# Row numbers between two layers at a wider pitch, output scatters declared independent, and products done by token half

## Chip, cores and metric

The kernel runs on 1 core of one Trainium2 chip. The metric is device time in microseconds (us), lower is better; each run gives the time of one execution. The profile is of one further execution, and its own time stands beside its span below.

## What is computed

Three layers in a row on 24,576 tokens of 256 numbers (8 sequences of 3,072), all float32:

```python
X = np.fft.rfft(x, axis=1)
Y = X * (filt_r + 1j * filt_i)[None, :, :]
x = np.fft.irfft(Y, n=3072, axis=1).reshape(24576, 256)

e_idx = np.argmax(x @ w_gate, axis=1)
for e in range(8):
    mask = e_idx == e
    h = np.maximum(x[mask] @ w1[e], 0.0)
    out[mask] = gate_w[mask, None] * eom[mask, e, None] * (h @ w2[e])

h = np.maximum(out @ w_in, 0.0)
return h * h @ w_out
```

The first is a filter in the frequency domain. The second is a layer of 8 experts (256 to 1,024 to 256), of which each token takes one. The third is a dense layer (256 to 2,048 to 256). The weights `w_in` and `w_out` of the third come as 64-bit numbers and are decoded on the chip.

## The kernel before

**Filter and routing** (up to about 750 us). The transform is done with matmuls; its last step also gives the routing scores. VectorE works out each token's expert and its place in that expert's list, and GpSimd scatters the token's row number to that place in one of four tables in HBM (`scatter`, L405: 128 numbers of 4 bytes in one DMA, each to its own place; the four tables are taken in turn). Tokens go to HBM as `yd`.

**Expert layer** (about 680 to 1965 us). The lists are cut into 62 tiles of one expert each: 41 wide ones of 512 tokens and 21 narrow ones of 256 (`width`). For each tile SP reads the list from the tables (`start_t`), GpSimd gathers the tokens (`gather`, L739), VectorE scales them (`scale_x`, L765), TensorE turns them (`turn_x`, L777, whose result ScalarE and VectorE split in two parts at L781 and L782), and `up` and `down` do the two products. All float32 products are done as three products of high and low parts. `load_w` brings expert weights from HBM, 512 KB for each quarter of a tile. The result of a tile goes to HBM transposed (`ytd`, L822), and with it the row numbers of its tokens (`idsc`, L823), so that the third layer can put each token's result in its row. A wide tile's 512 numbers are written as 128 runs of 4 (16 bytes), since slot 4p + c holds the number of token c * 128 + p. A narrow tile's 256 are written one by one, since its slot c * 128 + p holds token c * 128 + p. In both cases the numbers lie next to each other, 4 bytes apart.

**Decoding** runs beside the expert layer. `decode_all` is a generator that `step_1` moves on by one piece at six of every eight steps (L979). Each call of `decode` has SP load 256 KB of raw weights (`raw`, L612) and then works on VectorE, from L617 on. SP and VectorE take their instructions in program order, so a late load holds up all that stands behind L617 on VectorE.

**Dense layer** (about 1965 us to the end). 48 tiles of 512 columns of `ytd`, each in 8 units. `load_t` reads a tile and its row numbers (`ix`) more than one tile ahead; `split_t` splits the tile in high and low parts on ScalarE and VectorE (L859, L860) and forms sums of it (L868). The row numbers are read as four runs per partition; because narrow tiles were written in the other order, `split_t` takes the columns of the tiles from number 41 on with a step of four (`by`, L855). `up2` and `down2` do the products, interleaved in four parts per unit. `down2` sums a tile's four blocks of 128 tokens in two banks, `py0` for the first two blocks (k = 0) and `py1` for the others (k = 1):

```python
for m in range(24):
    i, k, c, n = m // 12, m // 6 % 2, m // 3 % 2, m % 3
```

so in each unit the banks take turns in groups of six matmuls. In a tile's last unit ScalarE copies a bank out (L934) when its last matmul, m = 17 or 23, is done, and GpSimd scatters its two blocks to their rows of the output (L937: 128 rows of 1 KB in a DMA). All of these scatters write the tensor `out`, and the framework, which cannot know that the rows differ, makes each wait until the one before has landed.

Of the kernel before, what the change touches and what calls it, by code (L numbers as in the profile page):

```python
# [11 lines left out]
F32 = mybir.dt.float32  # L12
F32R = mybir.dt.float32r
BF16 = mybir.dt.bfloat16
I32 = mybir.dt.int32
# [7 lines left out]
NT = B * S  # L23
# [8 lines left out]
TT = 512  # L32
# [9 lines left out]
NWIDE = KP + NTILE_L  # L42
# [58 lines left out]
def spectral_moe_kernel(ctx: ExitStack, tc: tile.TileContext, x, filt_r, filt_i, w_gate, w_og, w1, w2,  # L101
                        w_in, w_out, c_ma, c_mi, c_mb, c_mb2, c_sg, c_cum, out):
    nc = tc.nc
    ctx.enter_context(tc.manual_schedule())

    const = ctx.enter_context(tc.tile_pool(name="const", bufs=1))
# [2 lines left out]

    NTAB = 4  # L110
    ytd = dram.tile([D, NT + TT], F32, name="ytd")
    idsc = dram.tile([NT + TT, 1], I32, name="idsc")
    tab = [dram.tile([128 * TP, 1], I32, name=f"tab{i}") for i in range(NTAB)]
    tabv = [t.rearrange("(p c) o -> p (c o)", p=128) for t in tab]


# [36 lines left out]

    fft = ctx.enter_context(ExitStack())
    const.tile([128, 72], F32, name="pad")
    pl = {"xsm": ctx.enter_context(tc.tile_pool(name="xsm", bufs=2, side="right"))}
    right = lambda stack, name, bufs, **kw: stack.enter_context(tc.tile_pool(name=name, bufs=bufs, side="right", **kw))
    pl["xsm"].tile([128, 24], F32, name="xpad", bufs=1)  # L160
# [542 lines left out]
    slot, k = [], 0  # L703
# [102 lines left out]
    def down(t, f):  # L806
        hh, hl = H.pop((t, f))
        w = width[t]
        h2, l2 = (a[:, 1] for a in W[t, f // 2])
        if f == 0:  # L810
            Y[t] = [p[:, 0:w] for p in py_tiles(t)]
        for h in range(2):
            for i, (a, b) in enumerate(((h2, hh), (h2, hl), (l2, hh))):
                nc.tensor.matmul(Y[t][h], a[:, f % 2, h * 128:(h + 1) * 128], b,  # L814
                                 start=f == 0 and i == 0, stop=f == NF - 1 and i == 2)
        if f == NF - 1:
            yo = pl["yop1"].tile([128, 2, TT], F32, name="yt")[:, :, 0:w]
            for h, p in enumerate(Y.pop(t)):
                nc.scalar.copy(yo[:, h, :], p)
            c = cols.pop(t)  # L820
            idx = X[t][2][:, 0:w // 128]
            nc.sync.dma_start(out=ytd[:, ds(c, w)].rearrange("(h p) t -> p h t", p=128), in_=yo)  # L822
            nc.sync.dma_start(out=idsc[ds(c, w)].rearrange("(p c) o -> p (c o)" if w == TT else "(c p) o -> p (c o)", p=128), in_=idx)  # L823
            del X[t]
        if f % 2 == 1:
            w = W.pop((t, f // 2))
            if t + 1 < KP:
                W[t + 1, f // 2] = w
# [15 lines left out]
    def load_t(t):  # L844
        r = lpool[0].tile([128, 2, TT], F32, name="r")
        nc.sync.dma_start(out=r, in_=ytd[:, t * TT:(t + 1) * TT].rearrange("(h p) t -> p h t", p=128))
        ix = lpool[0].tile([128, 4], I32, name="ix")
        nc.sync.dma_start(out=ix, in_=idsc[t * TT:(t + 1) * TT].rearrange("(p c) o -> p (c o)", c=4))
        R[t] = r, ix

    def split_t(t):

        r, ix = R.pop(t)
        bh, bl = (pl["bp"].tile([128, 7, 256], F32R, name=n) for n in ("bh", "bl"))
        by = "p (c q) -> p c q" if t < NWIDE else "p (q c) -> p c q"  # L855
        rv = [[r[:, j].rearrange(by, c=4)[:, 2 * k:2 * k + 2] for k in range(2)] for j in range(2)]
        blk = lambda a: a.rearrange("p (c q) -> p c q", c=2)
        for i, (j, k) in enumerate(((0, 0), (1, 0), (1, 1))):
            nc.scalar.copy(blk(bh[:, i]), rv[j][k])  # L859
            nc.vector.tensor_tensor(blk(bl[:, i]), rv[j][k], blk(bh[:, i]).bitcast(F32), ALU.subtract)  # L860
        io = lpool[0].tile([128, 4], I32, name="io")
        nc.vector.tensor_scalar(io, ix, 1, None, op0=ALU.subtract)
        X2[t] = bh, bl, io
        yield
        b = pl["tp2"].tile([128, 4, 256], F32, name="tc")
        for i, (x, y) in enumerate(((rv[0][1], rv[0][0]), (rv[1][1], blk(b[:, 0])), (rv[1][1], rv[0][1]),
                                    (rv[1][0], blk(b[:, 1])))):
            nc.vector.tensor_tensor(blk(b[:, i]), x, y, ALU.subtract)  # L868
        yield
        nc.scalar.copy(bh[:, 3:7], b)  # L870
        yield
        nc.vector.tensor_tensor(bl[:, 3:7], b, bh[:, 3:7].bitcast(F32), ALU.subtract)
        yield
# [45 lines left out]
    def down2(t, u):  # L919
# [3 lines left out]
        if u == 0:  # L923
            Z[t] = [p.rearrange("p (c d) -> p c d", c=2) for p in py_tiles(t)]
        for m in range(24):
            i, k, c, n = m // 12, m // 6 % 2, m // 3 % 2, m % 3
            x, w = ((hh, woh), (hl, woh), (hh, wol))[n]
            nc.tensor.matmul(Z[t][k][:, c, :], x[:, 2 * i + k, c * 128:(c + 1) * 128], w[:, 2 * u + i, :],  # L928
                             start=u == 0 and m in (0, 6), stop=u == NU - 1 and m in (17, 23), skip_group_check=True)
            if u == NU - 1 and m in (17, 23):  # L930
                if k == 0:
                    Z[t].append(pl["oup"].tile([128, 4, D], F32, name="ou"))
                ou = Z[t][2]
                nc.scalar.copy(ou[:, 2 * k:2 * k + 2, :], Z[t][k])  # L934
                io = X2[t][2]
                for c in range(2 * k, 2 * k + 2):
                    nc.gpsimd.indirect_dma_start(out=out, out_offset=bass.IndirectOffsetOnAxis(ap=io[:, c:c + 1], axis=0),  # L937
                                                 in_=ou[:, c, :], in_offset=None)
            if m in (2, 8, 17):
                yield  # L940
        del H2[t, u]
# [196 lines left out]
```

## Time and profile before

| | us |
|---|---|
| time, median of 3 runs | 4010.77 (4009.82 to 4017.08) |
| the profiled execution: its time | 4012.15 |
| the profiled execution: its span | 4010.2 |
| TensorE busy (matmul) | 3841.1 |
| VectorE busy | 2836.9 |
| ScalarE busy | 2000.6 |
| GpSimd busy | 775.8 |

The span runs from the first to the last instruction of the program; 1.95 us of the profiled execution's time lie around it. Busy time alone says little here, because it is an average over three layers with different limits. In rows of the trace, PE is TensorE's matmuls, DVE VectorE, ACT ScalarE, POOL GpSimd, SP the queue that issues most DMAs; a number in square brackets at the end of a row is how long the engine had been idle, and after the arrow stands what ended it. The mean clock granted to TensorE was 0.982 of full speed over the span.

### The profile page before, as it was taken

The page shows a single profiled execution, that of the slowest core. Times are in us where ns is not written, and L with a number is a line of the kernel's source. Part 1 is how long each engine was busy: PE and PEld are TensorE (multiplying, and loading weights), DVE is VectorE, ACT ScalarE, POOL GpSimd, SP SyncE. Part 2 cuts the span into 40 slices and gives each one's busy share as a digit, 9 for nine tenths or more (in the row PEclk, how much of TensorE's full clock was granted, in tenths as well). Part 3 has the DMA queues.
Part 4 walks back from the last instruction along what each step waited for, and adds up shares of the span by engine and source line. Part 5 has one row for each costly group of instructions (what it writes and reads, how often), then busy time and mean ns, then how long its engine had stood idle before and what let it go on. Part 6 is the DMA issues. An engine that isn't in the chain of part 4 may idle for free.

```text
span 4010.2 us, 75055 instructions
## 1 busy us (share of the span) xinstructions
PE 3841.1 (96%) x27556; PEld 3573.5 (89%) x27556; DVE 2836.9 (71%) x5265; ACT 2000.6 (50%) x3957; POOL 775.8 (19%) x743
## 2 busy tenths in 40 slices
PE   8988897898999999999999999999999999999998
PEld 7777775687788888888899999999999999999998
DVE  7576675477788886666677777777777777777775
ACT  6364553244445445455455555555555555555554
POOL 3354545311111111211001011010110100101001
PEclk9999998999999999999999999999999999999999
DMA  6323222155666666666300000000000000000000
GB/s 222 105 78 114 89 75 72 59 151 145 154 155 175 172 161 164 158 159 162 100 22 28 28 25 30 22 28 28 24 28 26 27 28 23 27 27 26 29 17 17
DMA packets 270773, 318.74 MB, mean 79 GB/s; under 512 B 82082, under 2 KB 215427, under 8 KB 267331
## 3 DMA queue, kind: packets, MB, share of 16 engines
q1 hardware_dynamic: 244128, 259.71, 23.6%
q0 software_dynamic: 25248, 53.99, 4.5%
q8 instruction: 216, 3.54, 0.4%
q14 instruction: 155, 1.26, 0.1%
q10 hardware_dynamic: 1026, 0.23, 0.0%
HBM read 231.55 MB, written 82.26 MB: 78 GB/s over the span
## 4 chain that ended last, share of the span: by engine, by line
PE 87%; DVE 4%; DMA 3%; another core or an unknown queue 2%; issue 2%; ACT 1%; SPq 0%; POOL 0%; DVEq 0%; POOLq 0%; ACTq 0%
PE py L928 26%; PE ph L882 17%; PE ph L798 12%; PE py L814 12%; PE px L882 7%; PE o L357 3%; PE p L378 2%; PE o L392 2%; PE p L278 2%; PE p L331 1%; PE p L335 1%; PE p L306 1%; PE px L777 1%; DMA raw<-in_moe_w_in_dram 1%
## 5 line engine op out<-in xcount | busy, mean ns | idle before, releaser
L928 PE MATMUL py<-woh,hh 128*128 128x256 f32 x3072 | 857.1, 279 | 0.0
L928 PE MATMUL py<-woh,hl 128*128 128x256 f32 x3072 | 852.8, 278 | 0.4 <-DVE hl L915 0.4
L928 PE MATMUL py<-wol,hh 128*128 128x256 f32 x3072 | 852.9, 278 | 0.0
L928 PEld LDWEIGHTS py<-woh,hl 128*128 128x128 f32 x3072 | 579.8, 189 | 0.9 <-DVE hl L915 0.8
L928 PEld LDWEIGHTS py<-woh,hh 128*128 128x128 f32 x3072 | 579.9, 189 | 0.0
L928 PEld LDWEIGHTS py<-wol,hh 128*128 128x128 f32 x3072 | 576.3, 188 | 0.0
L937 POOL DMA_INDIRECT out_dram<-ou,io x192 | 207.9, 1083 | 1868.6 <-ACT C L904 1634.6
L802 ACT ACTIVATE hh<-ph 128x512 fp32r<-128x512 f32 (+1 forms) x496 | 261.2, 527 | 596.9 <-PE ph L798 537.8
L882 PE MATMUL ph<-bh,wsh 128*128 128x256 f32 x1920 | 542.1, 282 | 5.1 <-ACT s L889 2.7
L882 PE MATMUL ph<-bl,wsh 128*128 128x256 f32 x1920 | 537.6, 280 | 0.1
L882 PE MATMUL ph<-bh,wsl 128*128 128x256 f32 x1920 | 537.3, 280 | 0.0
L906 DVE SCALAR_TENSOR_TENSOR q<-C 128x1024 f32<-128x1024 f32 x384 | 470.2, 1224 | 1.9 <-ACT C L904 1.9
L915 DVE TENSOR_TENSOR hl<-q,hh 128x1024 fp32r<-128x1024 f32 x384 | 467.1, 1216 | 1.1 <-ACT hh L913 1.1
L803 DVE SCALAR_TENSOR_TENSOR hl<-ph,hh 128x512 fp32r<-128x512 f32 (+1 forms) x496 | 296.4, 598 | 232.5 <-ACT hh L802 205.8
L900 DVE TENSOR_TENSOR C<-ph,p 128x256 f32<-128x256 f32 x384 | 163.1, 425 | 399.7 <-ACT hh L913 397.4
L913 ACT CAST hh<-q 128x1024 fp32r<-128x1024 f32 x384 | 403.9, 1052 | 1.3 <-DVE q L906 1.3
L904 ACT COPY C<-ph 128x256 f32<-128x256 f32 x384 | 144.1, 375 | 501.2 <-PE ph L882 501.2
L739 POOL DMA_INDIRECT xg<-yd,idx x190 | 199.4, 1050 | 948.9 <-DVE idx L749 902.0
L882 PEld LDWEIGHTS ph<-bh,wsh 128*128 128x128 f32 x1920 | 362.4, 189 | 8.3 <-ACT s L889 4.1
L814 PE MATMUL py<-hh,wh 128*128 128x512 f32 (+1 forms) x992 | 363.4, 366 | 0.0
L882 PEld LDWEIGHTS ph<-bl,wsh 128*128 128x128 f32 x1920 | 360.8, 188 | 0.3 <-DVE bl L860 0.3
L882 PEld LDWEIGHTS ph<-bh,wsl 128*128 128x128 f32 x1920 | 360.9, 188 | 0.0
(267 smaller groups left out, 8772.1 us busy)
## 6 DMA issues: line engine op xcount, KB each, us to landing
r<-in_moe_w_dram SPq DMA_DIRECT2D x472, 256.0 KB
yd<-yo SPq DMA_DIRECT2D x24, 1088.0 KB
xt<-in_x_dram SPq DMA_DIRECT2D x48, 512.0 KB
r<-ytd SPq DMA_DIRECT2D x48, 512.0 KB
ytd<-yt SPq DMA_DIRECT2D x41, 512.0 KB
ytd<-yt SPq DMA_DIRECT2D x21, 256.0 KB
raw<-in_moe_w_in_dram SPq DMA_DIRECT2D x16, 256.0 KB
raw<-in_moe_w_out_dram SPq DMA_DIRECT2D x16, 256.0 KB
```

The costliest lines, as they stand in the source:

```text
L739: nc.gpsimd.indirect_dma_start(out=xg[:, c * YW:(c + 1) * YW], out_offset=None, in_=yd[0:(NT * GP // NG if t < KP else NT) + 1], in_offset ...
L798: nc.tensor.matmul(ps, a[:, c, f2 * 128:(f2 + 1) * 128], b[:, c, 0:w], start=n == 0, stop=n == 5)
L802: nc.scalar.activation(hh, ps, AF.Relu)
L803: nc.vector.scalar_tensor_tensor(hl, ps, 0.0, hh.bitcast(F32), op0=ALU.max, op1=ALU.subtract)
L814: nc.tensor.matmul(Y[t][h], a[:, f % 2, h * 128:(h + 1) * 128], b, start=f == 0 and i == 0, stop=f == NF - 1 and i == 2)
L882: nc.tensor.matmul(ps, x[:, u, a], y[:, b], start=start and n == 0, stop=n == 2, skip_group_check=True)
L900: nc.vector.tensor_tensor(C[:, 3], V, p5, ALU.add)
L906: nc.vector.scalar_tensor_tensor(q, C, 0.0, C, op0=ALU.max, op1=ALU.mult)
L913: nc.scalar.copy(hh, q)
L915: nc.vector.tensor_tensor(hl, q, hh.bitcast(F32), ALU.subtract)
L928: nc.tensor.matmul(Z[t][k][:, c, :], x[:, 2 * i + k, c * 128:(c + 1) * 128], w[:, 2 * u + i, :], start=u == 0 and m in (0, 6), stop=u == N ...
L937: nc.gpsimd.indirect_dma_start(out=out, out_offset=bass.IndirectOffsetOnAxis(ap=io[:, c:c + 1], axis=0), in_=ou[:, c, :], in_offset=None)
```

## The change

Three edits, and what they need:

- `idsc` gets 64 numbers (256 bytes) per row number and only the first of them is used. Wide and narrow tiles are now written in the same order, each number by itself. `load_t` reads them in that order, and `split_t` loses the step of four.
- In `down2` k is now the outermost of the loops, so a unit does all 12 matmuls of `py0` and then the 12 of `py1`; a bank is done at m = 11 and 23.
- The scatters to the output go through `apart`, which tells the framework that they don't depend on each other. It also issues one GpSimd memset of a single number behind each. (A pad is smaller by 32 bytes to make room for that number.)

```diff
-    idsc = dram.tile([NT + TT, 1], I32, name="idsc")
+    idsc = dram.tile([NT + TT, 64], I32, name="idsc")
+    def apart(key, i):
+        i = i.ins
+        nc.gpsimd.memset(spare, 0.0)
+        tc.declare_no_dep(i, group=key, reason="different rows")
+        tc.add_to_no_dep_group(key, i)
...
+    spare = const.tile([1, 1], F32, name="spare")
-    const.tile([128, 72], F32, name="pad")
+    const.tile([128, 64], F32, name="pad")
...
-            nc.sync.dma_start(out=idsc[ds(c, w)].rearrange("(p c) o -> p (c o)" if w == TT else "(c p) o -> p (c o)", p=128), in_=idx)
+            nc.sync.dma_start(out=idsc[ds(c, w), 0:1].rearrange("(c p) o -> p (c o)", p=128), in_=idx)
...
-        nc.sync.dma_start(out=ix, in_=idsc[t * TT:(t + 1) * TT].rearrange("(p c) o -> p (c o)", c=4))
+        nc.sync.dma_start(out=ix, in_=idsc[t * TT:(t + 1) * TT, 0:1].rearrange("(c p) o -> p (c o)", p=128))
...
-        by = "p (c q) -> p c q" if t < NWIDE else "p (q c) -> p c q"
-        rv = [[r[:, j].rearrange(by, c=4)[:, 2 * k:2 * k + 2] for k in range(2)] for j in range(2)]
+        rv = [[r[:, j].rearrange("p (c q) -> p c q", c=4)[:, 2 * k:2 * k + 2] for k in range(2)] for j in range(2)]
...
-            i, k, c, n = m // 12, m // 6 % 2, m // 3 % 2, m % 3
+            k, i, c, n = m // 12, m // 6 % 2, m // 3 % 2, m % 3
...
-                             start=u == 0 and m in (0, 6), stop=u == NU - 1 and m in (17, 23), skip_group_check=True)
-            if u == NU - 1 and m in (17, 23):
+                             start=u == 0 and m in (0, 12), stop=u == NU - 1 and m in (11, 23), skip_group_check=True)
+            if u == NU - 1 and m in (11, 23):
...
-                    nc.gpsimd.indirect_dma_start(out=out, out_offset=bass.IndirectOffsetOnAxis(ap=io[:, c:c + 1], axis=0),
-                                                 in_=ou[:, c, :], in_offset=None)
+                    apart("out", nc.gpsimd.indirect_dma_start(
+                        out=out, out_offset=bass.IndirectOffsetOnAxis(ap=io[:, c:c + 1], axis=0), in_=ou[:, c, :], in_offset=None))
```

The same instructions are issued in the same order on every engine, but for two places. The first is GpSimd at the end of the program: the last four scatters before, with the semaphores each waits for.

```order
L937 DMA out_dram<-ou,io 24576x256 [waits DMASW1_49,DVE_49,Activation_49]
L937 DMA out_dram<-ou,io 24576x256 [waits DMASW2_49]
L937 DMA out_dram<-ou,io 24576x256 [waits DMASW3_49,Activation_49]
L937 DMA out_dram<-ou,io 24576x256 [waits DMASW4_49]
L1133 UNCONDITIONAL_BRANCH
```

And now (L944 is L937 of before):

```order
L944 DMA out_dram<-ou,io 24576x256 [waits DMASW2_49,DVE_49,Activation_49]
L117 MEMSET spare 1x1 [waits Pool_49]
L944 DMA out_dram<-ou,io 24576x256 [waits DMASW3_49]
L117 MEMSET spare 1x1 [waits Pool_49]
L944 DMA out_dram<-ou,io 24576x256 [waits DMASW4_49,Activation_49]
L117 MEMSET spare 1x1 [waits Pool_49]
L944 DMA out_dram<-ou,io 24576x256 [waits DMASW5_49]
L117 MEMSET spare 1x1 [waits Pool_49]
L1140 UNCONDITIONAL_BRANCH
```

Both have a wait on a DMASW semaphore in each row, of which there are eight, used in turn. Before, it is the one that the scatter just ahead sets when it has landed; now it is the one that this scatter will set itself, last set by the scatter eight places ahead, that is two tiles earlier. The waits for ScalarE's copy (Activation) and for the row numbers (DVE) stay.

The second place is TensorE in each unit of `down2`, here matmuls 7 to 18 (m = 6 to 17) of the program's last unit, before. `py0` and `py1` are the banks, `hh2` and `hl2` the hidden values, `woh` and `wol` the weights.

```order
L928 MATMUL py1_48007<-woh_7574,hh2_48386 128x256
L928 MATMUL py1_48007<-woh_7574,hl2_48387 128x256
L928 MATMUL py1_48007<-wol_7575,hh2_48386 128x256
L928 MATMUL py1_48007<-woh_7574,hh2_48386 128x256
L928 MATMUL py1_48007<-woh_7574,hl2_48387 128x256
L928 MATMUL py1_48007<-wol_7575,hh2_48386 128x256
L928 MATMUL py0_48006<-woh_7574,hh2_48386 128x256
L928 MATMUL py0_48006<-woh_7574,hl2_48387 128x256
L928 MATMUL py0_48006<-wol_7575,hh2_48386 128x256
L928 MATMUL py0_48006<-woh_7574,hh2_48386 128x256
L928 MATMUL py0_48006<-woh_7574,hl2_48387 128x256
L928 MATMUL py0_48006<-wol_7575,hh2_48386 128x256
```

And now (L935 is L928 of before):

```order
L935 MATMUL py0_48195<-woh_7575,hh2_48575 128x256
L935 MATMUL py0_48195<-woh_7575,hl2_48576 128x256
L935 MATMUL py0_48195<-wol_7576,hh2_48575 128x256
L935 MATMUL py0_48195<-woh_7575,hh2_48575 128x256
L935 MATMUL py0_48195<-woh_7575,hl2_48576 128x256
L935 MATMUL py0_48195<-wol_7576,hh2_48575 128x256
L935 MATMUL py1_48196<-woh_7575,hh2_48575 128x256
L935 MATMUL py1_48196<-woh_7575,hl2_48576 128x256
L935 MATMUL py1_48196<-wol_7576,hh2_48575 128x256
L935 MATMUL py1_48196<-woh_7575,hh2_48575 128x256
L935 MATMUL py1_48196<-woh_7575,hl2_48576 128x256
L935 MATMUL py1_48196<-wol_7576,hh2_48575 128x256
```

The last matmul of `py0` has moved ahead by six places, and in the queues of ScalarE and GpSimd the copy and the scatters that follow it stand where they stood.

## Rows read from the trace of the kernel before

**Rows 1.** The page: the chain that ended last, by engine.

```profile
PE 87%; DVE 4%; DMA 3%; another core or an unknown queue 2%; issue 2%; ACT 1%; SPq 0%; POOL 0%; DVEq 0%; POOLq 0%; ACTq 0%
```

**Rows 2.** Waits of TensorE, 850 to 1960 us: total us, times, longest.

```profile
PE px L777 <- DVE xl L782: 26.9, 12, 7.6
```

**Rows 3.** Timeline of SP, 920 to 985 us: start, us, instruction.

```profile
940.10 0.66 SPq L612 DMA_DIRECT2D raw<-in_moe_w_in_dram  x1
...
958.03 0.39 SPq L823 DMA_DIRECT2D idsc<-idx  x1
958.52 0.48 SPq L612 DMA_DIRECT2D raw<-in_moe_w_in_dram  x1
```

**Rows 4.** Timeline of VectorE at the first steps of those two decodes.

```profile
945.58 0.29 DVE L617 TENSOR_SCALAR ea<-raw 128x256 int32<-128x256 int32 x1 [2.71 <-DMA raw<-in_moe_w_in_dram]
...
972.04 0.29 DVE L617 TENSOR_SCALAR ea<-raw 128x256 int32<-128x256 int32 x1 [9.99 <-DMA raw<-in_moe_w_in_dram]
```

**Rows 5.** Timeline of TensorE at its two longest waits there.

```profile
974.84 1.11 PE L777 MATMUL px<-ident,xs 128*128 128x128 f32 x4 [6.96 <-DVE xl L782]
...
1101.92 0.47 PE L777 MATMUL px<-ident,xs 128*128 128x128 f32 x1 [7.55 <-DVE xl L782]
```

**Rows 6.** Stretches: length, busy us of five engines, granted clock, DMA share, GB/s.

```profile
974.80:980.80 6.00, 5.96 (x16) 4.88 (x17) 4.46 (x9) 0.59 (x1) 1.54 (x2) 0.50 0.43 135
...
1101.90:1107.10 5.20, 5.18 (x14) 4.13 (x15) 4.23 (x9) 0.37 (x1) 3.78 (x4) 0.50 0.47 126
...
958.50:966.50 8.00, 8.00 (x39) 6.61 (x38) 3.21 (x7) 3.91 (x6) 0.00 (x0) 1.00 0.90 114
...
940.10:948.10 8.00, 4.84 (x41) 4.63 (x40) 4.72 (x14) 3.99 (x7) 0.37 (x1) 1.00 0.80 225
```

**Rows 7.** Timeline of SP at the end of the expert layer.

```profile
1965.86 0.37 SPq L823 DMA_DIRECT2D idsc<-idx  x1
1968.27 0.39 SPq L846 DMA_DIRECT2D r<-ytd  x1
1975.37 0.36 SPq L848 DMA_DIRECT2D ix<-idsc  x1
```

**Rows 8.** Waits of SP, 1965 to 1980 us: total us, times, longest.

```profile
SPq L848 <- DMA idsc<-idx: 6.7, 1, 6.7
```

**Rows 9.** Timeline of GpSimd, 690 to 712 us: row numbers to the tables.

```profile
699.71 1.00 POOL L405 DMA_INDIRECT tab<-rowid,si  x1 [0.31 <-issue]
...
704.83 0.96 POOL L405 DMA_INDIRECT tab<-rowid,si  x1 [0.30 <-issue]
```

**Rows 10.** Line 859, 1985 to 3640 us and 3640 us to the end: ns min/median/max.

```profile
L859 ACT CAST bh<-r x120: 407/408/410, 1989.5 to 3627.3; 128x256 fp32r<-128x256 f32 x120
...
L859 ACT CAST bh<-r x21: 652/672/681, 3668.5 to 3925.5; 128x256 fp32r<-128x256 f32 x21
```

**Rows 11.** Timeline of TensorE, 3666 to 3674 us.

```profile
3670.00 0.28 PE L882 MATMUL ph<-bh,wsl 128*128 128x256 f32 x1
3670.67 0.39 PE L882 MATMUL ph<-bh,wsh 128*128 128x256 f32 x1 [0.40 <-ACT s L889]
3670.90 0.28 PE L882 MATMUL ph<-bl,wsh 128*128 128x256 f32 x1
3671.01 0.29 PE L882 MATMUL ph<-bh,wsl 128*128 128x256 f32 x1
```

**Rows 12.** Timeline of GpSimd from 3985 us: first and last of the last four scatters.

```profile
3994.91 0.96 POOL L937 DMA_INDIRECT out_dram<-ou,io  x1 [28.23 <-ACT ou L934]
...
4003.41 0.96 POOL L937 DMA_INDIRECT out_dram<-ou,io  x1 [1.71 <-DMA out_dram<-ou,io]
```

**Rows 13.** Timeline of ScalarE there, and the chain in order of time.

```profile
3994.05 1.29 ACT L934 COPY ou<-py 128x512 f32<-128x512 f32 x2 [3.62 <-PE py L928]
...
3994.05 0.59 ACT ou L934
```

**Rows 14.** Groups of GpSimd: a memset of one number per partition (busy us, mean ns).

```profile
L1116 POOL MEMSET const-float32-0.0<- 128x1 f32 x1 | 0.1, 104 | 0.3 <-issue 0.3
```

## Prediction

> **What bounds the kernel now.** I read the page's chain first: 87% of what ended last is TensorE [rows 1]. So a change to another engine or a DMA is worth only the TensorE idle time or lost clock that it removes, or time after TensorE's last matmul. I then looked for those in TensorE's waits by stretch, and followed each wait back along the chain and the timelines of VectorE, SP and GpSimd. Three places remain that the change touches.
>
> First, 850 to 1960 us, the expert layer. TensorE waits 26.9 us in 12 pieces, all at the turning of a tile behind VectorE's split of the tile before [rows 2]. VectorE was not busy with it: it stood at the first step of a decode, waiting for raw weights. The reader is to see two such waits side by side. The raw load issued at 940.10, behind the row numbers of a wide tile, lets VectorE go on at 945.58, 5.5 us later, and holds it 2.71 us. The one issued at 958.52, 0.5 us behind the row numbers of a narrow tile, takes until 972.04, 13.5 us, and holds it 9.99 us [rows 3, 4]. In the 8 us behind the narrow write the DMA engines are as busy (0.90 against 0.80), yet move 114 GB/s against 225 [rows 6]. TensorE then idles 6.96 us, and once more 7.55 us at 1101.92, behind the next narrow write that a raw load follows at once [rows 5]. Behind each idle the granted clock is 0.50, the lower level of 1.2 GHz, for 6.0 and 5.2 us of busy matmuls [rows 6].
>
> The narrow write itself can be timed once. At 1965.86 one is issued; SP is held 6.7 us by it and goes on at 1975.37, so its 256 numbers took 9.5 us to land [rows 7, 8]. Four bytes each are not slow as such: the 128 four-byte numbers that a scatter puts far apart land within 5.1 us, because the next scatter to the same table, at 704.83 behind 699.71, was held by nothing but its issue [rows 9].
>
> Second, the splits of the last 7 dense tiles, with a step of four: their copy takes 672 ns against 408 [rows 10], and TensorE, which is otherwise without a gap there, waits for the copy queued behind it [rows 11].
>
> Third, the end: four scatters, each waiting for the one before to land, keep the program going from 3994.91 to past 4003.41 [rows 12].
>
> **The change, part by part.**
>
> *Row numbers.* Removed: the crowding of a narrow tile's 256 numbers in 1 KB. Added: a wide tile's numbers become 512 pieces instead of 128, and so do 48 reads. The new price, 256 or 512 pieces at 256 bytes, is in no row. Below, it is bounded by the scatter of rows 9, which shows no jam. Above, by the narrow write's 9.5 us per 256, or 37 ns a piece, for all pieces: 19 us for a wide write. I take the lower end, because the scatter is the nearer row: like the new write, it has one number in each stretch of memory, and crowding explains more of the trace. A narrow write puts 16 pieces in 64 bytes, a wide one 4. By a price per piece, a wide write of now, with 128, would jam for half as long as a narrow one; but the raw load behind it comes 8 us sooner, though twice the output data lies in front of it.
>
> Without the jam a raw load behind a narrow write should take what the one behind a wide write takes, 5.5 us. At 958.52 VectorE then waits 8.0 us less, 2 instead of 10. TensorE's 6.96 us go, and the slow stretch with them, since it followed the idle: half of 6.0 us, 3.0. At 1101.92 it is 7.55 and half of 5.2, 2.6. The sum is **20.1 us**. The other ten waits, 26.9 less 14.5, or 12.4 us, stand behind wide tiles, whose output is what delays the raw load most; I leave them at zero change, between 6 us less (half goes with the crowding) and 15 us more (1.5 us each for four times the pieces). What is late next after the two long waits is again the raw load, by some 2 us, which TensorE does not feel: its 6.96 are less than the 8.0 saved.
>
> The Trainium skill speaks against this part. "DMA: Bandwidth & Descriptors", section "Rules for kernel authors", says that a run which is not contiguous becomes one descriptor per element, and asks to make it contiguous; the change does the opposite for wide tiles. By that rule alone the wide waits would grow, toward the upper end above; by the rows the count of pieces is not what hurts, and the sum stays.
>
> The reads of row numbers are issued more than a tile ahead of `split_t`, which hides them; without that cover each would cost what it takes to land. SP issues as many DMAs as before, about 0.4 us each [rows 7], and nothing is moved past them.
>
> *Order of columns.* 7 splits lose the step of four, 3 copies of 672 ns becoming 408. TensorE's wait there is read from the starts: 3670.00 to 3670.67 to 3670.90, 0.90 us for two steps of 0.11, so 0.68 lost [rows 11]; 21 copies are 7 splits [rows 10]. **4.7 us**, nothing less in the other 41 tiles, where no such wait stands.
>
> *Products by token half.* No matmul more or less. Inside, the first copy and two scatters of a tile can start six matmuls earlier, and nothing waits for them: no gain. At the end `py0` is done six matmuls earlier, which is the distance of ScalarE's two copies, 1.29 less 0.59, 0.70 us [rows 13].
>
> *Independent scatters.* Also worth something only at the end. The first scatter starts at 3994.91 less 0.70, 3994.2. Two that wait for nothing start 0.96 to 1.00 plus 0.30 us apart [rows 9], and one memset of some 0.1 us comes in between [rows 14]: 1.4 us a step. The second copy, done at 3995.3, is ahead of the third scatter. So the last starts at about 3998.4 instead of 4003.41: **5.0 us**. What follows it (landing and the closing 6.8 us to the span's end) stays. If the memset held GpSimd until a scatter lands, the 5.0 would shrink to 0.7; it depends on another memset alone, so I don't take that. 192 memsets elsewhere lie in GpSimd's idle time.
>
> **Sum.** 20.1 + 4.7 + 5.0 = 29.8 us. The profiled execution took 4012.15 (span 4010.2 and 1.95 around it), so 3982.4 for its like; the median shown is 1.4 lower, which gives **3981 us**. A measurement of this kernel can tell about 0.2%, 8 us, from no change.
>
> **The rivals.**
>
> *Wide writes become the jam (slower).* Place: the 41 wide tiles. If a number costs 37 ns wherever it lies, a wide write lasts 19 us, and everything read behind it waits, as behind a narrow one. In the trace 10 us of VectorE's wait gave about 7 of TensorE idle and 3 of lost clock. By SP's timeline some nine wide tiles have a raw load within 2 us behind; with 13 us more delay each that is about 12 us a tile, 110 in all, less the 9.7 of the other parts: **4111 us**. It decides once a piece costs more than about 20 ns, for then the wide write outlasts the narrow one of now. For it: the price cannot be read before. Against it: rows 9, and the wide writes of now. The skill has a rule that would lead here by another road: "DMA: Bandwidth & Descriptors", section "Latency and other measured facts", has rows at a power-of-two pitch slowing each other, measured at far larger pitches; no run here shows it yet.
>
> *The pieces cost a little.* The ten waits behind wide tiles grow by 1.5 us each, the narrow jam goes: 3981 + 15 = **3996 us**. For it: four times the pieces on the same queue, ahead of the raw weights. Against: none of today's waits tells pieces from output data.
>
> *The jam stays.* If not the crowding but writing row numbers between two large transfers slows the reads, only 4.7 + 5.0 us go: **4001 us**. Against it: the transfer rate of rows 6, which differs between narrow and wide.
>
> *Wide waits shrink too.* Half of them goes, and the clock with it: **3974 us**.
>
> **How the numbers follow.** The forecast has 0.66, the wide jam 0.08, the small cost 0.13, the staying jam 0.06, the shrinking waits 0.07. The range is 3968 to 4002: it holds all but the wide jam and what lies outside by chance. Faster by over 0.2% means under 4002.7: all cases but the wide jam, and most of the staying jam, 0.89; I give 0.02 of that away for unknowns and put 0.87, within 0.2% 0.05, slower 0.08.
>
> **What would show it.** Right: VectorE's wait at the decodes of the two narrow tiles near 2 us, no clock of 0.50 behind them; behind the last narrow write `ix` issued within about 5 us of it; copies of 408 ns in all 48 splits and no wait of TensorE in the last 7; the last four scatters some 1.4 us apart. Wrong: a raw load of over 10 us behind wide tiles (first rival), TensorE's waits behind wide tiles over 12 us in sum (second), the two long waits still there (third), scatters still 2.7 us apart (the fourth edit does nothing).

## The result and the profile after

The changed kernel takes **3975.15 us** (median of 5 runs, 3967.52 to 3981.98) against 4010.77 (median of 5, 4005.17 to 4017.08) for the kernel before, a ratio of 0.991 with a 95% interval of 0.9893 to 0.9931. The profiled execution took 3973.72 us with a span of 3971.9 and a mean granted clock of 0.986, against 4012.15, 4010.2 and 0.982. A line of the changed kernel has a number 8 higher than before from L156 to L854, and 7 higher from L856 on: L612 is now L620, L777 is L785, L882 is L889.

The page's chain answers to [rows 1], TensorE's waits from 850 to 1960 us to [rows 2]:

```profile
PE 90%; DVE 3%; another core or an unknown queue 2%; DMA 2%; issue 1%; ACT 1%; SPq 0%; POOL 0%; DVEq 0%; POOLq 0%; ACTq 0%
```

```profile
PE px L785 <- DVE xl L790: 9.2, 11, 2.1
```

26.9 us of waiting in 12 pieces became 9.2 in 11, and the longest is 2.1 instead of 7.6. The timeline of SP has the same two pairs as [rows 3], a wide write and then a narrow one, each with its raw load close behind; below it are VectorE's first steps of the two decodes [rows 4]:

```profile
934.48 0.39 SPq L831 DMA_DIRECT2D idsc<-idx  x1
934.92 0.74 SPq L620 DMA_DIRECT2D raw<-in_moe_w_in_dram  x1
...
952.17 0.39 SPq L831 DMA_DIRECT2D idsc<-idx  x1
952.66 0.44 SPq L620 DMA_DIRECT2D raw<-in_moe_w_in_dram  x1
```

```profile
939.07 0.29 DVE L625 TENSOR_SCALAR ea<-raw 128x256 int32<-128x256 int32 x1 [1.43 <-DMA raw<-in_moe_w_in_dram]
...
957.05 0.29 DVE L625 TENSOR_SCALAR ea<-raw 128x256 int32<-128x256 int32 x1
```

Behind the wide write VectorE goes on 4.2 us after the issue (939.07 less 934.92; it was 5.5), behind the narrow one at most 4.4 us after it (it was 13.5), and there it does not wait at all. The first two rows are the turnings of TensorE that answer to [rows 5], and they have no wait now. The third is the longest wait that is left, and it stands one turning later, behind a wide tile:

```profile
962.77 0.60 PE L785 MATMUL px<-ident,xs 128*128 128x128 f32 x4
...
1079.27 0.38 PE L785 MATMUL px<-ident,xs 128*128 128x128 f32 x2
...
1096.98 0.66 PE L785 MATMUL px<-ident,xs 128*128 128x128 f32 x4 [2.10 <-DVE xl L790]
```

The stretches that answer to [rows 6] (length, busy us of PE, PEld, DVE, ACT and POOL, granted clock, DMA share, GB/s), first behind the two turnings, then behind the narrow write:

```profile
962.70:968.70 6.00, 6.00 (x29) 4.95 (x28) 4.18 (x8) 2.61 (x4) 0.00 (x0) 1.00 0.36 105
1079.20:1085.20 6.00, 6.00 (x31) 5.05 (x30) 4.81 (x9) 2.78 (x5) 2.75 (x3) 1.00 0.64 185
...
952.70:960.70 8.00, 8.00 (x39) 6.64 (x38) 6.33 (x17) 3.07 (x5) 0.94 (x1) 1.00 0.68 190
```

In the 8 us behind the narrow write the DMA engines now move 190 GB/s at a share of 0.68, against 114 at 0.90. The clock stays at 1.00 behind both turnings, where it was 0.50.

SP at the end of the expert layer [rows 7, 8]:

```profile
1936.20 0.38 SPq L831 DMA_DIRECT2D idsc<-idx  x1
1938.58 0.38 SPq L854 DMA_DIRECT2D r<-ytd  x1
1939.02 0.46 SPq L856 DMA_DIRECT2D ix<-idsc  x1
```

The read of the row numbers follows the write by 2.8 us, where it was 9.5, and SP's wait for `idsc` is gone. The copies of line 866, in the 40 dense tiles behind the first and in the last seven [rows 10], and TensorE's waits from 1985 us to the end, before and now:

```profile
L866 ACT CAST bh<-r x120: 405/408/410, 1961.3 to 3598.9; 128x256 fp32r<-128x256 f32 x120
...
L866 ACT CAST bh<-r x21: 405/408/408, 3640.3 to 3892.7; 128x256 fp32r<-128x256 f32 x21
```

```profile
PE ph L882 <- ACT s L889: 2.7, 7, 0.4
...
PE py L935 <- DVE hl L922: 0.5, 1, 0.5
```

All copies take 408 ns, and the seven waits at the splits [rows 11] are gone. Last, GpSimd's and ScalarE's end [rows 12, 13]:

```profile
3961.30 0.96 POOL L944 DMA_INDIRECT out_dram<-ou,io  x1 [32.76 <-ACT ou L941]
3962.26 0.09 POOL L117 MEMSET spare<- 1x1 f32 x1
3962.57 0.96 POOL L944 DMA_INDIRECT out_dram<-ou,io  x1 [0.22 <-issue]
...
3965.09 0.96 POOL L944 DMA_INDIRECT out_dram<-ou,io  x1 [0.21 <-issue]
```

```profile
3960.44 0.59 ACT L941 COPY ou<-py 128x512 f32<-128x512 f32 x1 [2.92 <-PE py L935]
3961.84 0.59 ACT L941 COPY ou<-py 128x512 f32<-128x512 f32 x1 [0.82 <-PE py L935]
```

First and last scatter start 3.79 us apart instead of 8.50, and the two copies 1.40 us apart instead of 0.70.

**Where the 38.3 us between the two spans went** can be read by setting the same instruction of both traces side by side. ScalarE's L802 (now L810), which makes the first hidden values of the expert layer, starts at 719.76 before and 715.12 after: 4.6 us are gained by then, in a part that the change does not touch. The first copy in [rows 10], that of the second dense tile, starts at 1989.5 and 1961.3, 28.2 apart, so the expert layer with the first dense tile gave 23.6. The last of the first 120 starts 28.4 apart and the last copy of all (3925.5 and 3892.7) 32.8, so the seven splits gave 4.4. The last scatter starts 38.3 apart, so the end gave 5.5.

### The profile page after: what moved, and what is told of

It is laid out like the page before. It is cut to its first block, busy times and chain, and to the rows that moved or that the text cites. A ratio compares the mean times of both kernels' runs of the same rounds, so it can differ in the third digit from the quotient of the medians.

```text
span 3971.9 us, 75245 instructions
## 1 busy us (share of the span) xinstructions
PE 3831.6 (96%) x27556; PEld 3569.5 (90%) x27556; DVE 2825.2 (71%) x5265; ACT 1993.5 (50%) x3957; POOL 793.8 (20%) x935
## 3 DMA queue, kind: packets, MB, share of 16 engines
q14 instruction: 155, 1.27, 0.1%
## 4 chain that ended last, share of the span: by engine, by line
PE 90%; DVE 3%; another core or an unknown queue 2%; DMA 2%; issue 1%; ACT 1%; SPq 0%; POOL 0%; DVEq 0%; POOLq 0%; ACTq 0%
PE py L935 27%; PE ph L889 17%; PE ph L806 13%; PE py L822 13%; PE px L889 7%; PE o L365 3%; PE p L386 2%; PE o L400 2%; PE p L286 2%; PE p L339 1%; PE p L343 1%; PE p L314 1%; PE px L785 1%; DVE hl L811 0%
## 5 line engine op out<-in xcount | busy, mean ns | idle before, releaser
L935 PE MATMUL py<-woh,hh 128*128 128x256 f32 x3072 | 857.2, 279 | 0.0
L935 PE MATMUL py<-woh,hl 128*128 128x256 f32 x3072 | 852.8, 278 | 0.5 <-DVE hl L922 0.5
L935 PE MATMUL py<-wol,hh 128*128 128x256 f32 x3072 | 852.9, 278 | 0.0
L944 POOL DMA_INDIRECT out_dram<-ou,io x192 | 213.8, 1114 | 1837.5 <-ACT ou L941 1805.1
L935 PEld LDWEIGHTS py<-woh,hl 128*128 128x128 f32 x3072 | 579.9, 189 | 1.0 <-DVE hl L922 0.9
L935 PEld LDWEIGHTS py<-woh,hh 128*128 128x128 f32 x3072 | 579.9, 189 | 0.0
L935 PEld LDWEIGHTS py<-wol,hh 128*128 128x128 f32 x3072 | 576.3, 188 | 0.0
L810 ACT ACTIVATE hh<-ph 128x512 fp32r<-128x512 f32 (+1 forms) x496 | 261.0, 526 | 598.9 <-PE ph L806 552.9
L889 PE MATMUL ph<-bh,wsh 128*128 128x256 f32 x1920 | 541.0, 282 | 1.9 <-DVE C L907 1.2
L889 PE MATMUL ph<-bl,wsh 128*128 128x256 f32 x1920 | 537.7, 280 | 0.1
L889 PE MATMUL ph<-bh,wsl 128*128 128x256 f32 x1920 | 537.2, 280 | 0.0
L913 DVE SCALAR_TENSOR_TENSOR q<-C 128x1024 f32<-128x1024 f32 x384 | 470.6, 1225 | 28.7 <-ACT C L911 28.7
L907 DVE TENSOR_TENSOR C<-ph,p 128x256 f32<-128x256 f32 x384 | 163.6, 426 | 401.3 <-ACT hh L920 398.3
L911 ACT COPY C<-ph 128x256 f32<-128x256 f32 x384 | 143.3, 373 | 558.6 <-PE ph L889 551.2
L889 PEld LDWEIGHTS ph<-bh,wsh 128*128 128x128 f32 x1920 | 362.9, 189 | 2.9 <-DVE C L907 1.7
L889 PEld LDWEIGHTS ph<-bl,wsh 128*128 128x128 f32 x1920 | 361.4, 188 | 0.3 <-DVE bl L867 0.3
L889 PEld LDWEIGHTS ph<-bh,wsl 128*128 128x128 f32 x1920 | 361.4, 188 | 0.0
```

The lines of the kernel that those rows point to most:

```text
L810: nc.scalar.activation(hh, ps, AF.Relu)
L889: nc.tensor.matmul(ps, x[:, u, a], y[:, b], start=start and n == 0, stop=n == 2, skip_group_check=True)
L907: nc.vector.tensor_tensor(C[:, 3], V, p5, ALU.add)
L913: nc.vector.scalar_tensor_tensor(q, C, 0.0, C, op0=ALU.max, op1=ALU.mult)
L944: apart("out", nc.gpsimd.indirect_dma_start(out=out, out_offset=bass.IndirectOffsetOnAxis(ap=io[:, c:c + 1], axis=0), in_=ou[:, c, :], in_ ...
```

## Experiments

The runs come from three chips, each with the kernel before beside it. The chips differ: the kernel before takes 3904.43 us on the first, 4008.37 on the second and 3906.11 on the third, so times are compared on one chip, and only traces and ratios across chips. Times in the expectations mostly go by the first measurement, where the kernel before takes 4010.77 us. No kernel here leaves work out. Where a time stands without a spread, the kernel was run once.

Two small things are needed to read the times. The expert layer, from its first hidden values (L802 before, L810 in the changed kernel) to the first copy of the dense layer, takes 1245.3 us in the trace of the kernel before and 1220.3 in that of the changed one. And a tile of the dense layer takes 41.97 us in the median in those two, but 41.87 in pitch16, mixed, pitch_alone and no_apart (read from its first scatter to that of the next tile), which is 4.7 us over the layer. Kernels with and without memsets, and with either order of products, have the shorter tile, so no edit here explains it, and its cause was not tried.

### First chip: what in the row numbers costs

**pitch4.** The changed kernel with its new order of row numbers, at the old distance:

```diff
-    idsc = dram.tile([NT + TT, 64], I32, name="idsc")
+    idsc = dram.tile([NT + TT, 1], I32, name="idsc")
```

> The changed kernel with its row numbers 4 bytes apart again, wide and narrow tiles both written one by one (wide: 512 pieces of 4 bytes next to each other). Theory (writes that fall into the same short stretch of memory follow each other slowly; what counts is how many pieces share a stretch): a wide write now has as many pieces in 64 bytes as a narrow one, so both kinds jam alike, for about 9.5 us, and raw loads close behind wide tiles take 12 to 14 us as well; some ten long waits of TensorE instead of two, time about 4040 to 4080 us. Rival (a price of about 37 ns for each adjacent piece, one after the other): a wide write lasts 19 us, twice the narrow one; raw loads behind wide tiles take over 20 us, time over 4100 us. Rival (the pitch is not what helped, the uniform order did): no jam, about 3975 us.

Measured: 4000.41 us, 96 **more** than the kernel before. TensorE's waits in the expert layer (610 to 1961 us on this chip), then the 8 us behind a raw load that follows a **wide** write at 1027.84 us, VectorE at the decode that this load feeds, and TensorE at the turning behind it:

```profile
PE px L785 <- DVE xl L790: 43.8, 14, 9.9
PE ph L806 <- ACT wh L764: 31.5, 13, 3.5
```

```profile
1028.33:1036.33 8.00, 4.87 (x41) 4.67 (x40) 2.26 (x5) 4.00 (x7) 0.00 (x0) 1.00 0.71 89
```

```profile
1040.59 0.29 DVE L625 TENSOR_SCALAR ea<-raw 128x256 int32<-128x256 int32 x1 [9.53 <-DMA raw<-in_moe_w_in_dram]
```

```profile
1043.13 1.12 PE L785 MATMUL px<-ident,xs 128*128 128x128 f32 x4 [9.93 <-DVE xl L790]
```

The DMA engines move 89 GB/s, where they moved 225 behind a wide write before [rows 6], and VectorE goes on 12.3 us after the issue, where it was 5.5. So wide writes jam too now, and the jam delays expert weights as well (the row with `wh`). This is the first rival's jam, at 4 bytes' distance. The landing of a write can be followed by the semaphore events of the trace: before the change the narrow writes take 9.2 to 11.3 us (median 10.0) and the wide ones 2.4 to 5.1 (3.7); in pitch4 the narrow ones take 7.2 to 11.1 (9.3) and the wide ones 8.6 to 12.9 (10.8). Twice the numbers do not take twice as long, so it is no price of 37 ns per number either. The 96 us are more than this theory's 30 to 70 over the kernel before, which had no waits for expert weights in it.

**pitch16** and **pitch64.** The same line with 4 numbers (16 bytes) per row number, and with 16 (64 bytes), where the changed kernel has 64 (256 bytes):

```diff
-    idsc = dram.tile([NT + TT, 64], I32, name="idsc")
+    idsc = dram.tile([NT + TT, 4], I32, name="idsc")
```

```diff
-    idsc = dram.tile([NT + TT, 64], I32, name="idsc")
+    idsc = dram.tile([NT + TT, 16], I32, name="idsc")
```

> The changed kernel with a pitch of 16 bytes. Theory (the count of pieces in 64 bytes, 4 here, as in a wide write of before): next to no jam, no wait of TensorE in the expert layer over 4 us, time 3975 to 3990 us. Rival (what counts is a stretch of 256 bytes, with 16 pieces here): about a quarter of the narrow tiles' jam and more of it on wide tiles, raw loads behind them of 7 to 8 us, time 3990 to 4020 us. Rival (a price per piece unless 256 bytes apart): as with 4 bytes, over 4040 us.

> The changed kernel with a pitch of 64 bytes. Theory (the count of pieces in 64 bytes, 1 here): the same as at 256 bytes, TensorE's waits behind the split of a tile 9 us in sum between 850 and 1960 us, time 3968 to 3982 us. Rival (a stretch of 256 bytes counts): a little jam left, waits of 10 to 20 us in sum, 3980 to 3995 us.

Measured: 3869.25 and 3867.13 us. TensorE's waits in the whole expert layer, first of pitch16, then of pitch64:

```profile
PE px L785 <- DVE xl L790: 13.3, 11, 5.4
```

```profile
PE px L785 <- DVE xl L790: 8.8, 11, 2.5
```

16 bytes of distance already take nearly all of it away. The two times cannot be told apart, but the expert layer takes 1221.5 us in pitch16 and 1214.6 in pitch64; the shorter dense tile of pitch16 hides this. In pitch64 the writes take 1.6 to 5.4 us, 3.3 in the median with 512 pieces and 3.7 with 256; in pitch16 both medians are above 4. So what costs is numbers, written one by one, that lie next to each other; the count of pieces does not.

**mixed.** Narrow tiles at 256 bytes, wide ones as before in runs of four, in a tensor of their own:

```diff
+    idsw = dram.tile([NT + TT, 1], I32, name="idsw")
...
-            nc.sync.dma_start(out=idsc[ds(c, w), 0:1].rearrange("(c p) o -> p (c o)", p=128), in_=idx)
+            nc.sync.dma_start(out=idsw[ds(c, w)].rearrange("(p c) o -> p (c o)", p=128) if w == TT else
+                              idsc[ds(c, w), 0:1].rearrange("(c p) o -> p (c o)", p=128), in_=idx)
```

> The changed kernel, but only narrow tiles write at 256 bytes; wide tiles write 128 runs of 4 numbers next to each other, as before, in a tensor of their own, and are read so. Theory (crowding): raw loads close behind wide tiles take 5.5 us again instead of about 4.1, TensorE's waits between 850 and 1960 us go from 9 to 12 us in sum, time 3975 to 3985 us, not to be told from the changed kernel. Rival (four times the pieces cost something): the wide waits fall below 9 us and the time is 3965 to 3972 us.

Measured: 3870.75 us (3865.26 to 3874.39), ratio 0.9918 (0.9901 to 0.9935). TensorE's waits in the whole expert layer; then VectorE behind the raw load of a wide tile, issued at 829.73 us in mixed and at 829.42 in pitch64:

```profile
PE px L786 <- DVE xl L791: 11.3, 11, 3.0
```

```profile
835.06 0.29 DVE L626 TENSOR_SCALAR ea<-raw 128x256 int32<-128x256 int32 x1 [2.57 <-DMA raw<-in_moe_w_in_dram]
```

```profile
832.79 0.29 DVE L625 TENSOR_SCALAR ea<-raw 128x256 int32<-128x256 int32 x1 [0.65 <-DMA raw<-in_moe_w_in_dram]
```

The time cannot be told from that of pitch64: the jam was in the narrow writes. The wide waits come back a little, as the theory had it. The raw load lets VectorE go on after 5.3 us, as in the kernel before, and after 3.4 in pitch64, and the waits are 11.3 us against 8.8. The expert layer takes 1217.3 us, 2.7 more than in pitch64. So four times the pieces cost nothing, and wide tiles seem to gain a few us by the change (one trace each).

### Second chip: the other edits

**pitch_alone.** Wider pitch and the order of columns; products and scatters as before (the diffs of no_apart and no_half together).

> Only the row numbers' part of the change: pitch of 256 bytes and uniform order; products and scatters as before. Theory: the expert layer's 20 to 22 us and the 4.5 us of the seven splits go, the end stays: 25 us faster than before, about 3986 us, last scatter 8.6 us behind the first as in the kernel before. Rival (the order of the products helps inside the dense layer as well): over 3990 us, with waits of TensorE left there.

Measured: 3978.5 us (3973.63 to 3981.27), ratio 0.9926 (0.9909 to 0.9942): 30 us less than the kernel before, where 25 were expected. Some 5 us of it are the shorter dense tile (41.87 us; old_raw_early, on the same chip, has 41.97), which cannot be put down to the edit, so about 25 come from the row numbers and what goes with them.

**no_apart.** The changed kernel with dependent scatters:

```diff
-                    apart("out", nc.gpsimd.indirect_dma_start(
-                        out=out, out_offset=bass.IndirectOffsetOnAxis(ap=io[:, c:c + 1], axis=0), in_=ou[:, c, :], in_offset=None))
+                    nc.gpsimd.indirect_dma_start(out=out, out_offset=bass.IndirectOffsetOnAxis(ap=io[:, c:c + 1], axis=0),
+                                                 in_=ou[:, c, :], in_offset=None)
```

> The changed kernel with scatters that wait for each other again (no memset either). Theory: the order of the products alone moves the first scatter forward by 0.7 us and the chain of four stays 8.5 us long; the last scatter starts 8 to 9 us behind the first instead of 3.8, the span ends 4 to 5 us later than with the scatters independent, all else alike. Rival (the memsets cost GpSimd or VectorE time in the dense layer): tiles of the dense layer get shorter than 41.97 us.

Measured: 3980.49 us. Its first and last scatter on GpSimd:

```profile
3963.30 0.96 POOL L944 DMA_INDIRECT out_dram<-ou,io  x1 [27.52 <-ACT ou L941]
...
3971.79 0.96 POOL L944 DMA_INDIRECT out_dram<-ou,io  x1 [1.70 <-DMA out_dram<-ou,io]
```

They are 8.49 us apart, as before, so the new order of products alone saves nothing between the scatters. What it can save is the start of the first one: that is 68.4 us behind the last split's copy, and 69.2 in pitch_alone, which has the old order. The term for the independence stands. The rival's shorter dense tile is there (41.87 us), but mixed has it too, with the memsets, so it does not speak for a price of the memsets.

**no_half.** The changed kernel with the old order of products:

```diff
-            k, i, c, n = m // 12, m // 6 % 2, m // 3 % 2, m % 3
+            i, k, c, n = m // 12, m // 6 % 2, m // 3 % 2, m % 3
```

> The changed kernel with the order of the products as before. Theory: the two copies of the last tile are 0.7 us apart instead of 1.4 and the first ends 0.7 us later; the four scatters are 1.27 us apart, so the last starts 0.7 us later against the last matmul; nothing else moves. Rival: the order of the products was worth more, and the last scatter starts over 1.5 us later against the last matmul.

Measured: 4010.12 us, 32 more than pitch_alone, which differs from it only in that its scatters are dependent and without memsets. A dense tile takes 42.74 us in the median, where nothing but the end of the program was expected to move. TensorE's waits from 1985 us on; then, in one tile, GpSimd's scatters and VectorE's next sum:

```profile
PE ph L889 <- issue: 21.5, 42, 0.5
```

```profile
2038.49 0.96 POOL L944 DMA_INDIRECT out_dram<-ou,io  x1 [37.15 <-ACT C L911]
2039.43 0.09 POOL L117 MEMSET spare<- 1x1 f32 x1
2039.75 0.96 POOL L944 DMA_INDIRECT out_dram<-ou,io  x1 [0.23 <-issue]
...
2042.27 0.96 POOL L944 DMA_INDIRECT out_dram<-ou,io  x1 [0.23 <-issue]
```

```profile
2042.88 0.42 DVE L907 TENSOR_TENSOR C<-ph,p 128x256 f32<-128x256 f32 x1 [2.31 <-PE ph L889]
```

In 42 of 48 tiles TensorE stands for 0.5 us, because VectorE's sum at L907 comes about 1 us late: it had been idle for 2.31 us (1.31 at the same place of a tile in no_half_again, below), and it starts while the fourth scatter is being issued. The product that it waited for was long done, so what held it is not in the profile. The changed kernel on the chip of its first profile shows the same lateness at another place, ScalarE's L911 (2.22 us idle instead of 1.49). It is no single event there either: VectorE's L913 waits 42 times for this copy, 25.3 us in all, against 6 times and 1.2 us in both_again. TensorE shows no wait for it.

**old_raw_early.** The kernel **before**, with each raw load issued one piece of the decode earlier:

```diff
+        if nxt is not None:
+            load_raw(pool, nxt)
```

> The kernel before, with crowded row numbers, but each decode's raw load issued one piece of the decoding earlier (before the last piece of the decode ahead, which no longer reads the buffer). Theory (the jam costs only through the raw load that VectorE waits for): the two long waits shrink or go although the narrow writes jam as before; 12 to 22 us faster than before, 3988 to 3999 us. Rival (the jam costs by itself, through expert weights or gathers that come late): less than 8 us faster, with waits of TensorE at other places behind narrow tiles.

Measured: 3983.44 us (3975.84 to 3992.75), ratio 0.9936 (0.9919 to 0.9952). TensorE's waits in the expert layer:

```profile
PE px L789 <- DVE xl L794: 6.3, 11, 1.6
```

The narrow writes are still crowded, and the waits go all the same. The gain is 25 us, a little above what was expected, and the expert layer takes 1216.5 us, no more than in the changed kernel. So in this kernel the crowding cost time only through the raw load that came too soon behind it.

### Third chip: the order of products again, and what is left

**both_again** is the changed kernel, beside the other three.

> The changed kernel once more, so that the three kernels beside it have it on the same chip. Expected: 0.991 of the kernel before (0.9893 to 0.9931 in its first measurement), and no wait of TensorE in the dense layer but the one at its end.

Measured: 3865.92 us (3863.84 to 3869.57), ratio 0.9896 (0.988 to 0.9913).

**no_half_again.**

> The changed kernel with the old order of products (banks in turns of six matmuls), measured once before at one look, where it took as long as the kernel before. Theory A (independent scatters one close behind the other delay the start of VectorE's sum at L907 by about 1 us in each dense tile, which the old order turns into 0.5 us of TensorE idle and as much again behind it, 0.75 us a tile): 48 tiles by 0.75 give 35 us over the changed kernel, so about 1.000 of the kernel before. Theory B (that one look was a disturbance): as the changed kernel, 0.991.

Measured: 3867.77 us (3862.75 to 3870.03), ratio 0.9896 (0.988 to 0.9913): as both_again. Scatters and memsets are as far apart as in no_half, but VectorE's sum behind them is on time, and TensorE has no wait but the one at the end:

```profile
2059.01 0.42 DVE L907 TENSOR_TENSOR C<-ph,p 128x256 f32<-128x256 f32 x1 [1.31 <-ACT hh L920]
```

```profile
PE py L935 <- DVE hl L922: 0.4, 1, 0.4
```

Theory A fails here. Theory B is unlikely, since 42 equal waits at one place do not look like a passing disturbance. The lateness goes with the chip, or with something else that changed between these runs, which neither theory had in it. no_half was run only once on the second chip, so this stays open.

**memset_dep.** Old order, memsets kept, scatters dependent:

```diff
         nc.gpsimd.memset(spare, 0.0)
-        tc.declare_no_dep(i, group=key, reason="different rows")
-        tc.add_to_no_dep_group(key, i)
```

> As no_half_again (old order of products), with the memsets behind the scatters kept, but the scatters no longer declared independent, so each waits again for the one before to land. If the memset is what delays VectorE (both engines want the same port), the wait of 0.5 us per dense tile stays: about 1.000 of the kernel before. If it is the scatters that follow each other closely, the wait goes with their distance: 0.992 to 0.993, as with the wider pitch alone.

Measured: 3870.19 us (3868.83 to 3876.09), ratio 0.9911 (0.9895 to 0.9928). It shows no such wait, but on this chip no kernel does, so it decides nothing between memset and scatters. It is 4.3 us above both_again in the medians; the last scatters alone, 8.5 us from first to last again, would make 4.7 to 5.4.

**raw_early_new.** The changed kernel with the edit of old_raw_early.

> The changed kernel with each raw load issued one piece of the decode earlier. If what is left of TensorE's waits in the expert layer (9.2 us in 11) is still VectorE waiting for raw weights, most of it goes: 6 to 9 us under the changed kernel, 0.989 of the kernel before. If those waits have another cause (VectorE's own work ahead of the split), they stay and the time is that of the changed kernel, 0.991.

Measured: 3860.17 us (3858.22 to 3861.66), ratio 0.9879 (0.9862 to 0.9895). This is the fastest kernel of the study, 5.7 us under both_again in the medians, and no run of the one overlaps the runs of the other. TensorE's waits in the whole expert layer, first of both_again, then of raw_early_new:

```profile
PE px L785 <- DVE xl L790: 9.5, 11, 2.2
```

```profile
PE px L797 <- DVE xl L802: 5.9, 11, 1.6
```

VectorE's waits for raw weights, 9.7 us for `w_out` and 9.5 for `w_in` in both_again, are gone altogether, yet TensorE still waits 5.9 us. So only a part of what was left was due to the raw weights, and "most of it goes" was too much.

## Why the prediction was right, point by point

The forecast was 3981 us, the result 3975.15, inside the range and on the side that was forecast. Of the parts of the sum, 29.8 us were forecast and 33.5 found.

*Row numbers: right in mechanism and nearly in size.* 20.1 us were forecast and the expert layer gave 23.6. The two long waits and the half clock behind them went as described, VectorE's wait behind the two narrow writes to nothing and to 1.5 us, where 2 were forecast. The 3.2 us of the ten other waits (12.4 less 9.2) were set at zero; they make up most of the difference, about half of the 6.2 that the fourth rival had. The prediction put the wide tiles between 6 us less and 15 more; the single numbers at a distance let the raw load behind them land sooner, and mixed, which takes this away, waits longer again, so the second rival's price of the pieces is not there. The choice of the lower end for the price of a piece held: 512 pieces at 256 bytes land in 3.3 us in the median. pitch4 is 96 us above the kernel before, as the first rival was 100, but not by its price: its wide writes take 10.8 us and not 19, and part of its time is waits for expert weights. The rule of the Trainium skill that spoke against this part, on runs that are not contiguous ("DMA: Bandwidth & Descriptors", section "Rules for kernel authors"), would have kept wide runs of 16 bytes. By mixed these are no better, and rather a few us worse, than single numbers at a distance. The cost that the rule warns of is there in pitch4, where wide numbers written one by one lie next to each other, and does not arise with a distance between them.

*Order of columns: right.* 4.7 forecast, 4.4 found.

*Independent scatters: right.* 5.0 forecast. A step is 1.27 us, not 1.4, since the idle time in front of a scatter is 0.21 and not 0.30. With the earlier start of the first scatter the end gave 5.5.

*Products by token half: the step that left something out.* The prediction gave it nothing inside the layer, since nothing waits for the earlier copy, and 0.70 us at the end. The end is as forecast: the first scatter starts 33.6 us earlier than before, the last split 32.8, which is 0.8. Inside, the step left out that the third edit brings four scatters close together in every tile. On the second chip these cost 32 us with the old order (one run of no_half, against pitch_alone), and on the chip of the first measurement, where a copy is late in the same way, no wait of TensorE shows with the new order. The new order was not run beside no_half on the second chip. I had costed each edit beside the kernel before, not beside the other edits; "also worth something only at the end" held for the scatters because the new order came with them. The sum came out right because the change contains both, and that was luck.

*What the sum did not contain.* 4.6 us of the profiled difference arose before the expert layer. The filter's instructions are unchanged, and why they ran faster there was not tried. The five runs of one kernel lie up to 14.5 us apart, so that the result is nearer to the fourth rival's 3974 us than to the forecast says little.

## What to carry to other kernels

Do not put a stream of 4-byte writes next to each other in front of a load that somebody waits for: give each number a place of its own (16 bytes were nearly enough here), or write runs of them, or issue the load ahead of it. When several edits go in together, cost each in the kernel that has the others. And profile the same kernel on more than one chip before putting a stall down to an edit.

## What was not expected of the hardware

The same kernel takes 107.4 us less span in both_again (3864.5) than in its first profile (3971.9). Nearly all of it, 100.6 us, lies before the first hidden values of the expert layer (715.1 us against 614.5), where GpSimd scatters row numbers to the tables, many in a row. TensorE idles 108 us of this part in the first profile and 35 in both_again; the rest is busy time at a lower clock. In the first profile the other engines stop during a run of 14. GpSimd, ScalarE, VectorE and TensorE there:

```profile
275.55 0.96 POOL L413 DMA_INDIRECT tab<-rowid,si  x1 [0.31 <-issue]
...
284.39 0.96 POOL L413 DMA_INDIRECT tab<-rowid,si  x1 [0.30 <-issue]
```

```profile
276.66 0.58 ACT L288 COPY big<-p 128x512 f32<-128x512 f32 x1 [3.53 <-PE o L400]
286.53 0.39 ACT L389 COPY vt<-p 128x272 f32<-128x272 f32 x1 [9.29 <-remote]
```

```profile
282.26 0.69 DVE L288 COPY big<-p 128x512 f32<-128x512 f32 x1 [7.70 <-remote]
```

```profile
288.39 1.27 PE L400 MATMUL o<-vt,m 128*128 128x272 f32 x2 [10.56 <-ACT yo L401]
```

In both_again the same run of 14 scatters passes with ScalarE at work beside it. Two rows, of GpSimd and of ScalarE, stand for it:

```profile
265.29 0.96 POOL L413 DMA_INDIRECT tab<-rowid,si  x1 [0.30 <-issue]
...
265.71 0.39 ACT L389 COPY vt<-p 128x272 f32<-128x272 f32 x1 [0.74 <-PE p L386]
```

TensorE's wait for `yo` behind ScalarE, from 100 to 700 us, is 26.8 us in the first profile and 1.9 in both_again. ScalarE's waits that no instruction of this core ends ("remote"), up to 715 us in the first profile, are

```profile
ACT vt L389 <- remote: 44.2, 5, 12.3
ACT big L288 <- remote: 25.9, 4, 6.8
```

and both_again has none. In their first 720 us, all traces of the first measurement and of the second chip have such waits, and no trace of the first and the third chip has one. That fits the 1 us of no_half: in the runs here, where the kernel before takes 4008 to 4011 us, other engines start late while GpSimd issues scatters close behind each other, and where it takes 3904 to 3906 they do not. The runs in the filter have no memset between them, which speaks against the memset as the cause. The Trainium skill names a port that VectorE and GpSimd hold against each other ("SBUF — State Buffer", section "SBUF: two separate sides"); by that page TensorE and ScalarE have ports of their own, and they stop here too. What holds them, and whether it is the scatters at all, stays open, and so does why it differs between the chips. Spreading the filter's scatters out was not tried.
